# Downsampled attention values in 64x64 tiles of TensorE beside the local values in PSUM

## The chip, the cores and the metric

One core of one Trainium2 chip runs the whole program. The metric is device time in microseconds (us): the median of several executions of one kernel. The five engines that appear below are TensorE (PE; PEld is its loading of weights), VectorE (DVE), ScalarE (ACT), GpSimd (POOL) and SyncE (SP, which issues transfers).

## The reference

q, k and v have 8 batches, 8 heads, 576 positions and 64 columns. Two attentions are computed for each head and added: one over the means of 4 neighbouring positions (144 by 144), repeated 4 times, and one in which a position sees only positions at a distance below 4. A gated layer follows.

```
q_d, k_d, v_d = means of 4 rows            # 144 x 64 for each head
out_up    = repeat(softmax(q_d k_d' / 8) v_d, 4)
out_local = softmax(where(|i-j| < 4, q k' / 8, -1e9)) v
x = (out_up + out_local), heads side by side  # 8 x 576 x 512
h = relu(x @ w_in); u, v = halves of h     # w_in 512 x 1024
v_n = (v - mean) / sqrt(var + 1e-6)
v_s = w_spatial @ v_n + b_spatial          # over positions, 576 x 576
out = (u * v_s) @ w_out                    # w_out 512 x 512
```

## The kernel before

A step of attention, `attention(n)`, handles one pair of heads of one batch; there are 32 steps, n = 0 to 31, four for each batch. The two heads lie on partitions 0-63 and 64-127. After every four steps `gated(b)` lays out the gated layer of a batch, whose matmuls use all 128 rows and columns of the array in fp16 pairs of a high and a low part (batch 0 in fp32).

The pieces of one step on TensorE, with the names that the program gives them:

- S (line 875): 20 fp32 matmuls of 64 columns in the four 64x64 tiles of the array, the local scores. Where the mask is added on TensorE, four matmuls of line 868 precede them; otherwise VectorE adds it (line 888).
- Sd (line 922): 6 fp32 matmuls of 144 columns, the downsampled scores. A tile is diagonal where head h writes its own half of the partitions and off-diagonal where it writes the other half. Row block a = 0 and a = 1 use the two diagonal tiles, a = 2 the two off-diagonal ones; they are issued in the order 0, 2, 1.
- T (line 951) turns the local probabilities, Td (line 1013) the downsampled ones in fp16: nine matmuls with 112 moving columns.
- AV (line 1062): 20 fp32 matmuls of about 58 columns in 64x64 tiles, the local values, into the PSUM tile `pv`. Blocks 0, 2 and 4 use diagonal tiles, blocks 1 and 3 off-diagonal ones.
- AVd (line 1051): the downsampled values of batches 1 to 7, 10 fp16 matmuls with 96 rows and 64 columns of weights and 144 moving columns, five for each half of the output partitions, into the PSUM tile `pw`, a bank from the pool `pm` that the gated layer uses too.

ScalarE copies `pw` with a scale to `dn` (line 1084), VectorE adds it to `pv` (`both`, lines 1072 and 1074).

The order of all instructions is worked out before anything is emitted: class `Plan` keeps a list of pieces with a cost, a list `ORDER` of numbers that rank them, and a string per kind of choice in `ON` that says which engine takes it. `run` places the pieces by these, and each engine then runs its list in that order. From step 8 on, S, Sd of one step and AV, AVd of the step before are forced to follow each other without a gap (`first.next`, `second.next`, `av.next`); there are 24 such units. Below, such four pieces are called a unit, and Q, H and F are the ways in which the array is divided: 64x64 tiles, column halves, and whole. `TURN` holds the planner's cost of passing from one to another.

Of the kernel before, what the change touches and what calls it, by code (L numbers as in the profile page):

```python
# [76 lines left out]
class Plan:  # L77
# [64 lines left out]
    def run(self, near=150.0, stay=0.0, dma=(1500.0, 4.2, 500.0), emit=True):  # L142

        free = {}
        todo = {}
# [9 lines left out]
        for o in self.ops:  # L155
            free.setdefault(o.eng, 0.0)
            todo.setdefault(o.eng, [])
            if not o.wait:
                todo[o.eng].append(o)
# [264 lines left out]
MB = 8  # L424


ON = {"shrink": "AAAAAAADA",
      "sum": "PPDPDPDDPDDDPDPDDPPDDPPDPPDPPPDP",
      "mask": "TTTTTTDTDDTDDTDDDDTTD",
      "norm": "DPPPDPPDDPDPDDDDDPPDDDDPDDDPPPD",  # L430
# [923 lines left out]
```

## Time and profile before

| what | value |
|---|---|
| median of 3 runs | 568.89 us (568.71 to 569.19) |
| span of the profiled execution | 568.2 us |
| PE busy | 547.3 us, 96% of the span |
| DVE, ACT, POOL busy | 445.1, 362.8, 138.6 us |
| granted PE clock, mean | 0.979 of 2.4 GHz |

The page gives the profiled execution by its span alone, from the first to the last instruction; no other time of that execution is recorded, so its own time is taken as the span and stands 0.7 us below the median of the three runs. The span has three parts: up to about 68 us the inputs and weights come in and the first four steps run, to about 500 us attention and the gated layer are interleaved, and the rest is the gated layer of the last batch alone. A busy engine is not one at its peak; for TensorE the distance from the start of one piece to the start of the next is read, since records of consecutive matmuls overlap.

### The profile page before, as it was taken

The numbers are of one execution on the slowest core, as the hardware profiler recorded it, in microseconds if no ns is written. First come the engines' busy times: TensorE is split into PE (matmuls) and PEld (weight loads), VectorE is DVE, ScalarE is ACT, GpSimd is POOL, SyncE is SP. The second block draws the span as 40 slices with busy tenths as digits, with TensorE's granted clock in tenths as the row PEclk, the third lists the DMA queues.
The fourth block names the chain that finished last, engine by engine and source line by source line (L and its number), as shares of the span: only waits on it lengthen the run. The fifth ranks groups of instructions, "written<-read, shape, count | busy, mean of one in ns | idle before, by whom it ended". The sixth has DMA issues, their size and how long they took to land.

```text
span 568.2 us, 15639 instructions
## 1 busy us (share of the span) xinstructions
PE 547.3 (96%) x6312; PEld 368.1 (65%) x6312; DVE 445.1 (78%) x1222; ACT 362.8 (64%) x925; POOL 138.6 (24%) x163
## 2 busy tenths in 40 slices
PE   5878799999999999999999999999999999999997
PEld 2556367766777576766678566766767666865573
DVE  5789998996999888795799699899968878833350
ACT  4768787776775687555767678557755776544422
POOL 6314332201621123201521135203502132001300
PEclk9669899999999999999999999999999999999999
DMA  9999844215460445315342345332550410100102
GB/s 237 259 251 287 197 86 136 76 45 152 98 149 9 150 108 107 104 50 174 60 110 67 122 108 127 103 114 87 109 136 7 126 44 2 39 20 0 49 9 92
DMA packets 40467, 59.76 MB, mean 105 GB/s; under 512 B 4042, under 2 KB 27210, under 8 KB 40396
## 3 DMA queue, kind: packets, MB, share of 16 engines
q1 hardware_dynamic: 38092, 51.69, 31.5%
q0 software_dynamic: 2304, 7.08, 7.9%
q8 instruction: 49, 0.80, 0.7%
q14 instruction: 22, 0.18, 0.1%
HBM read 46.57 MB, written 9.44 MB: 99 GB/s over the span
## 4 chain that ended last, share of the span: by engine, by line
PE 81%; DVE 7%; DMA 7%; ACT 2%; POOL 1%; issue 1%; SPq 0%; ACTq 0%; DVEq 0%; POOLq 0%
PE pma L1257 5%; PE pmb L1220 5%; PE pmd L1220 5%; PE pmc L1257 5%; PE pmd L1257 4%; PE pma L1131 4%; PE pmb L1131 4%; PE pmd L1198 4%; PE pmb L1198 4%; PE pmc L1220 4%; PE pma L1220 3%; PE pmd L1131 3%; PE pma L1198 3%; PE pmc L1198 3%; PE pmb L1257 2%; PE pab L1062 2%
## 5 line engine op out<-in xcount | busy, mean ns | idle before, releaser
L1220 PEld LDWEIGHTS <-vha 128*128 128x128 f16 x768 | 73.7, 98 | 19.4
L1198 PEld LDWEIGHTS <-win 128*128 128x128 f16 x672 | 64.7, 98 | 18.8
L1257 PEld LDWEIGHTS <-more 128*128 128x128 f16 x192 | 18.6, 98 | 20.8
L1257 PEld LDWEIGHTS <-g 128*128 128x128 f16 x192 | 18.3, 98 | 20.4
L1220 PE MATMUL pmb<-wsp,vha 128*128 128x256 f16 (+1 forms) x228 | 30.9, 285 | 0.0
L1220 PE MATMUL pmd<-wsp,vha 128*128 128x256 f16 (+1 forms) x216 | 29.5, 286 | 0.0
L846 POOL TENSOR_TENSOR suma<-qkb 128x576 f32<-128x576 f32 x9 | 11.6, 1286 | 52.2 <-DMA qkb<-qk_dram 52.2
L1220 PE MATMUL pmc<-wsp,vha 128*128 128x320 f16 (+1 forms) x168 | 23.6, 290 | 0.0
L1162 POOL TENSOR_TENSOR stc<-stc,mhalf 128x1 f32<-128x1 f32 (+1 forms) x13 | 9.8, 753 | 54.6 <-DVE stc L1143 54.4
L846 POOL TENSOR_TENSOR suma<-qka 128x576 f32<-128x576 f32 x8 | 9.8, 1225 | 54.3 <-DMA qka<-qk_dram 50.3
L1162 POOL TENSOR_TENSOR stb<-stb,mhalf 128x1 f32<-128x1 f32 (+1 forms) x13 | 12.1, 934 | 44.5 <-DVE stb L1143 44.5
L1220 PE MATMUL pma<-wsp,vha 128*128 128x256 f16 (+1 forms) x156 | 20.8, 283 | 0.0
L943 POOL TENSOR_TENSOR sb<-sb,smb 128x640 f32<-128x640 f32 x9 | 12.3, 1364 | 28.0 <-DVE smb L910 17.2
L1162 POOL TENSOR_TENSOR sta<-sta,mhalf 128x1 f32<-128x1 f32 (+1 forms) x14 | 9.9, 705 | 28.8 <-DVE sta L1143 28.7
L1257 PE MATMUL pmd<-wo,g 128*128 128x512 f16 x72 | 16.5, 380 | 0.0
L1257 PE MATMUL pma<-wo,more 128*128 128x512 f16 x72 | 16.5, 379 | 0.0
L980 DVE SCALAR_TENSOR_TENSOR eh<-eda,smda,eh 128x144 f16<-128x144 f32 x42 | 15.9, 443 | 0.1
L980 DVE SCALAR_TENSOR_TENSOR wst<-edb,smdb,wst 128x144 f16<-128x144 f32 x42 | 15.0, 419 | 1.1 <-ACT wst L974 1.1
L765 POOL DMA_DIRECT2D tv<-v_dram x12 | 11.6, 970 | 14.1 <-DMA tv<-v_dram 13.9
L1131 PEld LDWEIGHTS <-xa 128*128 128x128 f16 x84 | 8.2, 98 | 9.9
L939 ACT ACTIVATE sa<-sa 128x640 f32<-128x640 f32 x16 | 11.8, 734 | 4.2 <-DVE sa L903 3.2
L939 ACT ACTIVATE sb<-sb 128x640 f32<-128x640 f32 x16 | 11.8, 738 | 3.4 <-DVE sb L894 1.8
(1051 smaller groups left out, 1713.1 us busy)
## 6 DMA issues: line engine op xcount, KB each, us to landing
qka<-qk_dram SPq DMA_DIRECT2D x16, 576.0 KB, 3.9
qkb<-qk_dram SPq DMA_DIRECT2D x16, 576.0 KB
tv<-v_dram POOLq DMA_DIRECT2D x12, 288.0 KB, 5.6
wst<-v_dram POOLq DMA_DIRECT2D x12, 288.0 KB, 5.0
stg<-w_in_dram SPq DMA_DIRECT2D x6, 512.0 KB, 6.2
out_dram<-rowa SPq DMA_DIRECT2D x8, 256.0 KB, 2.0
out_dram<-rowd SPq DMA_DIRECT2D x8, 256.0 KB, 4.9
out_dram<-rowc SPq DMA_DIRECT2D x7, 256.0 KB, 2.0
```

What stands on the lines that cost most here:

```text
L765: plan.op("POOL", 850, lambda r=r: nc.gpsimd.dma_start(t.ap, v4[b, r], accum_op=ALU.add), w=[t], rank=rank + 2.0 + 0.3 * r, kb=288, name="tv")
L846: side(s1).tensor_tensor(sb.ap.rearrange("p x (g r) -> p x g r", r=2), x[:, :, :, :2], x[:, :, :, 2:], op=ALU.add)
L939: exp_of.append(plan.op("ACT", 643, lambda: nc.scalar.activation(s.ap, s.ap, AF.Exp, scale=1.0 / 8.0), w=[s], rank=R["E"], name="exp"))
L943: plan.op(nm, 0, lambda: side(nm).tensor_tensor(s.ap, s.ap, sm.ap[:, :, None].broadcast_to([P, NW, 64]), op=ALU.mult), r=[sm], w=[s], rank ...
L980: nc.vector.scalar_tensor_tensor(eh.ap[:, a, :, 1], ed.ap[:, a, :], smd.ap[:, a:a + 1], eh.ap[:, a, :, 0], op0=ALU.mult, op1=ALU.subtract)
L1062: nc.tensor.matmul(pv.ap[h * 64:h * 64 + 64, c:c + QB[w + 1] - QB[w]], vb.ap[k, w], pT.ap[k, blk, q0:q0 + QB[w + 1] - QB[w]], start=True, ...
L1131: nc.tensor.matmul(ps.ap, xs[c].ap[:, i, t * P:(t + 1) * P], win[:, c, j, FF:], start=(c == 0 and (i, j) == (0, 0)), stop=(c == NC - 1 and ...
L1162: plan.op("POOL", 830, lambda: nc.gpsimd.tensor_tensor(st.ap[:r, 8:9], st.ap[:r, 8:9], mhalf[:r], op=ALU.pow), w=[st], rank=rank - EVICT, ...
L1198: nc.tensor.matmul(ps.ap[:, :n], win[:, c, i, ft * P:(ft + 1) * P], xs[c].ap[:, j, HA[h]:HA[h + 1]], start=(c == 0 and (i, j) == (0, 0)), ...
L1220: nc.tensor.matmul(ps.ap[:, :n], vh.ap[:, c, i, fs], wsp[:, c, j, hs], start=(c == 0 and (i, j) == (0, 0)), stop=False)
L1257: nc.tensor.matmul(ps.ap, g.ap[:, c, i, k:k + P] if t < NT else gt.ap[:, c, i], wo[:, c, j, :], start=(c == 0 and (i, j) == (0, 0)), stop= ...
```

## The change

The downsampled values are computed in 64x64 tiles, in four partial products: rows 0-63 and rows 64 up of the transposed probabilities meet their own half of `th` (now on 128 partitions, with another layout of rows), so that 16 matmuls take the place of 10. They write into the PSUM tile `pv`, at columns that the local values leave free: diagonal products into its first bank, off-diagonal ones into its second. A new VectorE instruction adds the second half to `dn`. In Sd, a = 1 and a = 2 are both off-diagonal and the order is 0, 1, 2. In a unit, AV has another order of blocks. Td transposes pieces with 128 instead of 96 weight columns. All numbers of `ORDER` and most choices in `ON` are new: 6 instead of 11 steps add the mask on TensorE (none of them in a unit; before, 4 were), 12 instead of 19 local normalisations and 11 instead of 19 low parts of v (line 1168) run on VectorE, the rest on POOL.

```diff
-            for a in (0, 2, 1):
+            for a in range(3):
...
-                    c = h ^ (a == 2)
+                    c = h ^ (a > 0)
...
-                    x = eh.ap[:112, a, 96:].rearrange("p k x -> p (k x)") if c == 1 else eh.ap[:112, a, :96, c // 2]
+                    x = eh.ap[:112, a, :P, c] if c < 2 else eh.ap[:112, a, 80:].rearrange("p k x -> p (k x)")
...
-        pw, dn = plan.buf("pm"), plan.buf("dn")
+        dn = plan.buf("dn")
+        def part_d(bank):
+            at = 512 * bank + (3 - bank) * BLK - 4 * (1 - bank)
+            return pv.ap[:, at:at + G]
...
-            passes = ((0, 0), (2, 0), (0, 2), (1, 1), (1, 3))
-            for i, (c, k) in enumerate(passes):
-                for h in range(2):
-                    nc.tensor.matmul(pw.ap[h * 64:h * 64 + 64, :G], w[:, k, p, h * D:h * D + D], t[:, c, :, h, :],
-                                     start=i == 0, stop=i == len(passes) - 1)
+            for i, (c, k) in enumerate(((0, 0), (0, 1), (1, 0), (2, 2), (2, 3))):
+                for cross_tile in range(2):
+                    for h in range(2):
+                        r = h ^ cross_tile
+                        if c == 2 and not r:
+                            continue
+                        rows = slice(64, P if c == 2 else 112) if r else slice(64)
+                        nc.tensor.matmul(part_d(cross_tile)[h * 64:h * 64 + 64], w[rows, k, p, h * D:h * D + D], t[rows, c, :, h, :],
+                                         start=i == 0, stop=i == (4 if r else 2))
...
+            if chained:
+                order = [(0, 0), (0, 1), (2, 0), (1, 0), (2, 1), (1, 1), (4, 0), (3, 0), (4, 1), (3, 1)]
...
+            if not whole:
+                plan.op("DVE", 220, lambda: nc.vector.scalar_tensor_tensor(dn.ap, part_d(1), sx_of[b][0].ap[:, 11:12], dn.ap, op0=ALU.mult, op1=ALU.add),
...
-      "mask": "TTTTTTDTDDTDDTDDDDTTD",
-      "norm": "DPPPDPPDDPDPDDDDDPPDDDDPDDDPPPD",
+      "mask": "DDTTTTTTDDDDDDDDDDDDDDDDDDDDDDDD",
+      "norm": "PPDPDPPPDDPPDPPPPPDPPDPPDDDPPDDP",
```

What the change does to the order is shown at two places. The first is TensorE's list at a unit in the middle of the program, before; L875 is S, L922 Sd, L1062 AV and L1051 AVd, whose pairs repeat to ten:

```order
L875 MATMUL paa<-qka 64x64 x20
L922 MATMUL pmc<-kda 64x144 x2
L922 MATMUL pmd<-kda 64x144 x2
L922 MATMUL pmc<-kda 64x144 x2
L1062 MATMUL pab<-probTb,vd 64x60 x2
L1062 MATMUL pab<-probTb,vd 64x58 x2
L1062 MATMUL pab<-probTb,vd 64x56 x2
L1062 MATMUL pab<-probTb,vd 64x58 x10
L1062 MATMUL pab<-probTb,vd 64x54 x2
L1062 MATMUL pab<-probTb,vd 64x58 x2
L1051 LDWEIGHTS wst
L1051 MATMUL pma<-pdTa,wst 64x144
```

The same unit in the changed kernel, where L900 is S, L947 Sd, L1101 AV and L1085 AVd, whose pairs repeat to sixteen:

```order
L900 MATMUL paa<-qka 64x64 x20
L947 MATMUL pma<-kda 64x144 x2
L947 MATMUL pmb<-kda 64x144 x4
L1101 MATMUL pab<-probTb,vd 64x60 x2
L1101 MATMUL pab<-probTb,vd 64x56 x2
L1101 MATMUL pab<-probTb,vd 64x58 x8
L1101 MATMUL pab<-probTb,vd 64x54 x2
L1101 MATMUL pab<-probTb,vd 64x58 x6
L1085 LDWEIGHTS wst
L1085 MATMUL pab<-pdTa,wst 64x144
L1085 LDWEIGHTS wst
L1085 MATMUL pab<-pdTa,wst 64x144
```

Sd now ends with two pairs into one bank, the off-diagonal ones, AV begins with three blocks of diagonal tiles (columns 60, 56 and 58), and AVd stays with the tile `pab` that AV writes.

The second place is VectorE's list behind a unit, before; L888 adds the mask of the new step, L925 to L927 and L891 take maxima, L1072 and L1074 add `dn` to the local values of the older step:

```order
L888 TENSOR_TENSOR sa<-paa,mask 128x2x3x64
L888 TENSOR_TENSOR sa<-paa,mask 128x2x2x64
L925 TENSOR_REDUCE mxda<-pmb 128x2
L926 TENSOR_REDUCE mxda<-pma 128x1
L927 TENSOR_SCALAR mxda<-mxda 128x3
L891 TENSOR_REDUCE mxa<-sa 128x10
L1072 TENSOR_TENSOR xfa<-pab,dnb 128x2x116 x2
L1074 TENSOR_TENSOR xfa<-pab,dnb 128x112
L894 TENSOR_TENSOR sa<-sa,mxa 128x640
```

A like place in the changed kernel, where L913 adds the mask, L950 to L952 and L916 take maxima, L1127 is the new instruction and L1111 and L1113 add `dn`:

```order
L913 TENSOR_TENSOR sb<-pab,mask 128x2x3x64
L913 TENSOR_TENSOR sb<-pab,mask 128x2x2x64
L950 TENSOR_REDUCE mxdb<-pmc 128x1
L951 TENSOR_REDUCE mxdb<-pma 128x2
L952 TENSOR_SCALAR mxdb<-mxdb 128x3
L916 TENSOR_REDUCE mxb<-sb 128x10
L1127 SCALAR_TENSOR_TENSOR dna<-paa,sxb,dna 128x144
L919 TENSOR_TENSOR sb<-sb,mxb 128x640
L1111 TENSOR_TENSOR xfb<-paa,dna 128x2x116 x2
L1113 TENSOR_TENSOR xfb<-paa,dna 128x112
```

The new instruction stands between a maximum and the subtraction (L919) that needs that maximum; what follows it in the list waits until it has run.

## Rows read from the trace of the kernel before

**Rows 1.** The page, part 1: busy time of each engine.
```profile
PE 547.3 (96%) x6312; PEld 368.1 (65%) x6312; DVE 445.1 (78%) x1222; ACT 362.8 (64%) x925; POOL 138.6 (24%) x163
```

**Rows 2.** The page, part 4: the chain that ended last, by engine.
```profile
PE 81%; DVE 7%; DMA 7%; ACT 2%; POOL 1%; issue 1%; SPq 0%; ACTq 0%; DVEq 0%; POOLq 0%
```

**Rows 3.** Busy time by stretch: length, PE, PEld, DVE, ACT, POOL, PEclk, DMA share, GB/s.
```profile
40.00:68.00 28.00, 23.32 (x273) 14.80 (x274) 27.23 (x75) 21.33 (x61) 8.62 (x10) 0.93 0.96 263
...
250.00:350.00 100.00, 99.60 (x1259) 68.17 (x1252) 82.41 (x225) 68.33 (x180) 28.42 (x30) 1.00 0.44 113
...
78.00:568.20 490.20, 485.02 (x5620) 330.48 (x5618) 381.18 (x1056) 309.41 (x782) 109.38 (x112) 1.00 0.32 85
```

**Rows 4.** PE's waits from 78 us on, the two longest of four: total, times, longest.
```profile
PE pmb L571 <- ACT junk L730: 0.4, 1, 0.4
PE pmb L1013 <- DVE eh L980: 0.4, 1, 0.4
```

**Rows 5.** Timeline of PE, the first unit: start, length, what, records; then the last unit's ends.
```profile
123.64 0.81 PE L875 MATMUL paa<-qka 64*64 64x64 f32 x40
124.28 0.29 PE L922 MATMUL pmb<-kda 64*64 64x144 f32 x2
...
124.52 0.29 PE L922 MATMUL pmb<-kda 64*64 64x144 f32 x2
124.54 0.33 PE L1062 MATMUL pab<-probTb,va 64*64 64x58 f32 x4
...
124.77 0.86 PE L1062 MATMUL pab<-probTb,va 64*64 64x60 f32 x36
125.56 0.50 PE L1051 MATMUL pma<-pdTa,th 96*64 96x144 f16 x10
125.99 0.82 PE L1257 MATMUL pmc<-wo,more 128*128 128x512 f16 x3
...
484.56 0.81 PE L875 MATMUL paa<-qkb 64*64 64x64 f32 x40
...
486.91 0.83 PE L1220 MATMUL pmc<-wsp,vha 128*128 128x256 f16 x6
```

**Rows 6.** Timeline of PE, a unit with the mask: its first piece and what follows it.
```profile
153.05 0.33 PE L868 MATMUL pab<-mask_b,mask_a 64*64 64x320 bf16 x4
...
155.51 0.58 PE L1198 MATMUL pmd<-xe,win 128*128 128x320 f16 x3
```

**Rows 7.** Timeline of PE, AV and AVd of the last step, outside a unit.
```profile
497.95 0.91 PE L1062 MATMUL paa<-probTb,vd 64*64 64x60 f32 x40
498.79 0.50 PE L1051 MATMUL pmd<-pdTa,th 96*64 96x144 f16 x10
499.22 0.99 PE L1220 MATMUL pma<-wsp,vha 128*128 128x320 f16 x6
```

**Rows 8.** Timeline of PE, the first of a Td's nine matmuls and what follows them.
```profile
320.02 0.26 PE L1013 MATMUL pmc<-ident,eh 112*96 112x112 f16 x2
...
320.46 0.39 PE L1198 MATMUL pmd<-xb,win 128*128 128x256 f16 x2
```

**Rows 9.** Groups by line and form, DVE and POOL: count, busy us, mean ns, idle before.
```profile
L980 DVE SCALAR_TENSOR_TENSOR eh<-eda,smda,eh 128x144 f16<-128x144 f32 x42 | 15.9, 443 | 0.1
L943 DVE TENSOR_TENSOR sa<-sa,sma 128x640 f32<-128x640 f32 x12 | 10.1, 844 | 0.2
...
L888 DVE TENSOR_TENSOR sa<-paa,mask 128x384 f32<-128x384 f32 x8 | 4.4, 548 | 0.6 <-PE paa L875 0.4
...
L926 DVE TENSOR_REDUCE mxdb<-pmc 128x1 f32<-128x144 f32 x6 | 1.8, 298 | 0.0
...
L943 POOL TENSOR_TENSOR sb<-sb,smb 128x640 f32<-128x640 f32 x9 | 12.3, 1364 | 28.0 <-DVE smb L910 17.2 <-PE paa L875 6.0 <-DVE kda L849 4.7
```

**Rows 10.** PE's waits over the whole span, the longest.
```profile
PE pab L951 <- POOL sb L943: 3.1, 1, 3.1
```

**Rows 11.** ScalarE's copy to `dn` (line 1084): idle before it, until when, and how often.
```profile
  PE pma L1051: 12.9, 10
```

More of the change, by code (lines that the diff above doesn't have):

```diff
@@ L142, in run @@
     def run(self, near=150.0, stay=0.0, dma=(1500.0, 4.2, 500.0), emit=True):
-        free = {}
-        todo = {}
+        free = dict.fromkeys(("SP", "DVE", "ACT", "PE", "POOL"), 0.0)
+        todo = {e: [] for e in free}
         port = 0.0
@@ L155, in run @@
         for o in self.ops:
-            free.setdefault(o.eng, 0.0)
-            todo.setdefault(o.eng, [])
             if not o.wait:
@@ L424 @@
 MB = 8
-ON = {"shrink": "AAAAAAADA",
-      "sum": "PPDPDPDDPDDDPDPDDPPDDPPDPPDPPPDP",
-      "mask": "TTTTTTDTDDTDDTDDDDTTD",
-      "norm": "DPPPDPPDDPDPDDDDDPPDDDDPDDDPPPD",
-      "normd": "PDAAPAAAPPAPAAAPAADAAADDDAAAAAAD",
-      "vlo": "DPDDDDPDDDDPDPDDPDPDDPPDDDPDDDDPPDDDPDP"}
+ON = {"shrink": "ADAAAADDAADA",
+      "sum": "PDDPPPPDPPDDPPPPDDPDDPDPPPDDDDDP",
+      "mask": "DDTTTTTTDDDDDDDDDDDDDDDDDDDDDDDD",
+      "norm": "PPDPDPPPDDPPDPPPPPDPPDPPDDDPPDDP",
+      "normd": "PAAAAAAAPPAPAADPAADAADAPAPAADAAP",
+      "vlo": "PPDPDPPDPDDPPDDDPDDDPPDDDPPDPDPPPPDPPPD"}
 @with_exitstack
@@ L518, in tile_kernel @@
     plan.tag("tv", [old[:72, :2 * FF].rearrange("p (j d) -> p j d", j=NP), tv1])
-    th1 = const.tile([96, 4, NP, 2 * D], F16, name="th1")
-    plan.tag("th", [old[:96, 2 * FF:4 * FF].bitcast(F16).rearrange("p (c j d) -> p c j d", c=4, j=NP), th1])
+    th1 = const.tile([P, 4, NP, 2 * D], F16, name="th1")
+    plan.tag("th", [old[:, 2 * FF:4 * FF].bitcast(F16).rearrange("p (c j d) -> p c j d", c=4, j=NP), th1])
     places("tx", 1, [72, 4, NP, 2 * D], F16)
@@ L534, in tile_kernel @@
     places("smd", 2, [P, 3], F32)
-    places("pdT", 1, [96, 2, 3, 96], F32)
+    places("pdT", 1, [P, 2, 3, 96], F32)
     places("dn", 2, [P, G], F32)
@@ L812, in spread_rows @@
         def spread_rows():
-            a, z = th.ap[:, ::2], tx.ap
-            for dst, src in ((a[:72], z[:, ::2]), (a[72:], z[:24, 1::2]), (th.ap[0:96:2, 1::2], z[24:, 1::2]), (th.ap[1:96:2, 1::2], z[24:, 1::2])):
+            a, z = th.ap, tx.ap
+            for dst, src in ((a[:72, :2], z[:, ::2]), (a[72:112, :2], z[:40, 1::2]), (a[64::2, 2:], z[40:, 1::2]), (a[65::2, 2:], z[40:, 1::2])):
                 nc.sync.dma_start(dst, src)
@@ L913, in down @@
         def down(a):
-            return pd[a // 2].ap[:, (a % 2) * G:(a % 2) * G + G]
+            return pd[min(a, 1)].ap[:, a // 2 * G:a // 2 * G + G]
         def scores_d():
             q = kb.ap.rearrange("p x g -> p (x g)")
-            for a in (0, 2, 1):
+            for a in range(3):
                 for h in range(2):
                     r = slice(h * 64, h * 64 + 64)
-                    c = h ^ (a == 2)
+                    c = h ^ (a > 0)
                     nc.tensor.matmul(down(a)[c * 64:c * 64 + 64], q[r, 48 * a:48 * a + 64], kb.ap[r, 1], start=True, stop=True)
         def maximum_d():
-            nc.vector.tensor_reduce(mxd.ap[:, :2], pd[0].ap[:, :2 * G].rearrange("p (a k) -> p a k", a=2), axis=AX.X, op=ALU.max)
-            nc.vector.tensor_reduce(mxd.ap[:, 2:], down(2), axis=AX.X, op=ALU.max)
+            nc.vector.tensor_reduce(mxd.ap[:, :1], down(0), axis=AX.X, op=ALU.max)
+            nc.vector.tensor_reduce(mxd.ap[:, 1:], pd[1].ap[:, :2 * G].rearrange("p (a k) -> p a k", a=2), axis=AX.X, op=ALU.max)
             nc.vector.tensor_scalar(mxd.ap, mxd.ap, -1.0 / 128.0, None, op0=ALU.mult)
@@ L930, in attention @@
         first = plan.op(sc, 0, scores, r=[qkb], w=[ps], hold=[s, *([*pd, ed, *prev[1]] if prev else ())], after=prev[2] if prev else (), rank=R["S"], mode="Q", name="S")
-        second = plan.op("PE", 510, scores_d, r=[kb], w=list(pd), hold=[ed], after=[first] if prev else (), rank=R["Sd"], lag=PEL, mode="Q", name="Sd")
+        second = plan.op("PE", 330 if prev else 510, scores_d, r=[kb], w=list(pd), hold=[ed], after=[first] if prev else (), rank=R["Sd"], lag=PEL, mode="Q", name="Sd")
         if prev:
@@ L996, in turn_d @@
                 for a in range(3):
-                    nc.tensor.matmul(v[:, a, :112], ed.ap[:112, a, kc * 72:kc * 72 + n], cross if a == 2 else ident[:112, :112],
+                    nc.tensor.matmul(v[:, a, :112], ed.ap[:112, a, kc * 72:kc * 72 + n], cross if a else ident[:112, :112],
                                      start=True, stop=True, is_transpose=True)
@@ L1008, in turn_h @@
         def turn_h():
-            v = turned(ptd[0])[:96, :9 * 112].rearrange("p (c a q) -> p c a q", c=3, a=3)
+            v = turned(ptd[0])[:, :9 * 112].rearrange("p (c a q) -> p c a q", c=3, a=3)
             for c in range(3):
                 for a in range(3):
-                    x = eh.ap[:112, a, 96:].rearrange("p k x -> p (k x)") if c == 1 else eh.ap[:112, a, :96, c // 2]
-                    nc.tensor.matmul(v[:, c, a], x, cross16 if a == 2 else ident16, start=True, stop=True, is_transpose=True)
+                    x = eh.ap[:112, a, :P, c] if c < 2 else eh.ap[:112, a, 80:].rearrange("p k x -> p (k x)")
+                    nc.tensor.matmul(v[:, c, a], x, cross16 if a else ident16, start=True, stop=True, is_transpose=True)
         def half_t():
@@ L1019, in copy_h @@
             nc.scalar.copy(half_t().rearrange("p (c q) -> p c q", q=96),
-                           turned(ptd[0])[:96, :9 * 112].rearrange("p (c q) -> p c q", q=112)[:, :, :96])
+                           turned(ptd[0])[:, :9 * 112].rearrange("p (c q) -> p c q", q=112)[:, :, :96])
         copies = [copied]
@@ L1041, in values_d @@
                 for kc, n in enumerate(KEYS):
-                    nc.tensor.matmul(pw.ap[h * 64:h * 64 + 64, :G], tv.ap[:, p, (2 * kc + h) * D:(2 * kc + h + 1) * D], t[:n, kc, :, h, :],
+                    nc.tensor.matmul(part_d(0)[h * 64:h * 64 + 64], tv.ap[:, p, (2 * kc + h) * D:(2 * kc + h + 1) * D], t[:n, kc, :, h, :],
                                      start=(kc == 0), stop=(kc == 1))
@@ L1047, in values_h, with values @@
             w = th_of[b].ap
-            passes = ((0, 0), (2, 0), (0, 2), (1, 1), (1, 3))
-            for i, (c, k) in enumerate(passes):
-                for h in range(2):
-                    nc.tensor.matmul(pw.ap[h * 64:h * 64 + 64, :G], w[:, k, p, h * D:h * D + D], t[:, c, :, h, :],
-                                     start=i == 0, stop=i == len(passes) - 1)
-        def values():
-            order = [(blk, i, h) for j in range(0, NBLK, 2) for i in range(2) for blk in (j, j + 1) for h in range(2) if blk < NBLK]
-            for blk, i, h in order:
+            for i, (c, k) in enumerate(((0, 0), (0, 1), (1, 0), (2, 2), (2, 3))):
[7 more added lines that the diff above has]
+                                         start=i == 0, stop=i == (4 if r else 2))
+        def values(chained):
+            if chained:
+                order = [(0, 0), (0, 1), (2, 0), (1, 0), (2, 1), (1, 1), (4, 0), (3, 0), (4, 1), (3, 1)]
+            else:
+                order = [(blk, i) for j in range(0, NBLK, 2) for i in range(2) for blk in (j, j + 1) if blk < NBLK]
+            for blk, i, h in [(*o, h) for o in order for h in range(2)]:
                 w = 2 * blk + i
@@ L1077, in finish @@
         def finish(*after):
-            av = plan.op("PE", 675, values, r=[vb, pT], w=[pv], hold=[xf, x], after=after, rank=R["AV"], lag=PEL, mode="Q", name="AV")
-            avd = plan.op("PE", 450 if whole else 240, values_d if whole else values_h,
-                          r=[*((tv,) if whole else (th_of[b].sub(0),)), pdT.sub(0), pdT.sub(1)], w=[pw], hold=[dn], after=[av] if after else (), rank=R["AVd"], lag=PEL, mode="H", name="AVd")
+            av = plan.op("PE", 560 if after else 675, lambda: values(bool(after)), r=[vb, pT], w=[pv], hold=[xf, x], after=after, rank=R["AV"], lag=PEL, mode="Q", name="AV")
+            avd = plan.op("PE", 450 if whole else 190 if after else 260, values_d if whole else values_h,
+                          r=[*((tv,) if whole else (th_of[b].sub(0),)), pdT.sub(0), pdT.sub(1)], w=[pv.sub("d")], hold=[dn], after=[av] if after else (), rank=R["AVd"], lag=PEL,
+                          mode="H" if whole else "Q", name="AVd")
             if after:
                 av.next = avd
-            plan.op("ACT", 176, lambda: nc.scalar.copy(dn.ap, pw.ap[:, :G]) if whole else
-                    nc.scalar.activation(dn.ap, pw.ap[:, :G], AF.Copy, scale=sx_of[b][0].ap[:, 11:12]),
-                    r=[pw, *(() if whole else (sx_of[b][0].sub(10),))], w=[dn], rank=R["AVd"] - EVICT, name="dn")
-            plan.op("DVE", 795, both, r=[pv, dn], w=[x.sub(0) if whole else xf], rank=R["AV"] - EVICT, name="xf")
+            plan.op("ACT", 176, lambda: nc.scalar.copy(dn.ap, part_d(0)) if whole else
+                    nc.scalar.activation(dn.ap, part_d(0), AF.Copy, scale=sx_of[b][0].ap[:, 11:12]),
+                    r=[pv.sub("d"), *(() if whole else (sx_of[b][0].sub(10),))], w=[dn], rank=R["AVd"] - EVICT, name="dn")
+            if not whole:
+                plan.op("DVE", 220, lambda: nc.vector.scalar_tensor_tensor(dn.ap, part_d(1), sx_of[b][0].ap[:, 11:12], dn.ap, op0=ALU.mult, op1=ALU.add),
+                        r=[pv.sub("d"), sx_of[b][0].sub(10)], w=[dn], rank=R["AVd"] - EVICT, name="dn2")
+            plan.op("DVE", 795, both, r=[pv, pv.sub("d"), dn], w=[x.sub(0) if whole else xf], rank=R["AV"] - EVICT, name="xf")
             if whole:
```

273 rows, old and new, of the table ORDER are left out of this document.

## The prediction

> **What bounds the kernel now.** I read the busy times first: PE is busy for 96% of the span and the next engine, DVE, for 78% [rows 1]. A busy share alone proves nothing, so the chain that ended last comes second: 81% of it is PE's own work, 7% DVE and 7% transfers [rows 2]. Third, the stretches: from 78 us to the end PE is busy in 485.0 of 490.2 us, at a granted clock of 1.00 (the 2.4 GHz level) [rows 3], and its waits in all that time are four, the two longest 0.4 us each [rows 4]. The reader should see a queue that is never empty: there, a microsecond of work taken from PE is a microsecond of the span, until another engine falls behind. DVE, with 82.4 us in a steady 100 [rows 3], is the nearest. The stretch before differs: from 40 to 68 us DVE has 27.2 of 28 us and the transfers 0.96, and PE idles [rows 3].
>
> Last, PE's timeline gives the price of a unit [rows 5]. In the first one S starts at 123.64, Sd at 124.28, AV's main part at 124.77, AVd at 125.56 and the next piece at 125.99: 2.35 us. All 24 units cost the same (2.34 or 2.35 without mask, the last 484.56 to 486.91), and four of them add a mask, 153.05 to 155.51, 2.46 us [rows 6]. So one number times 24 carries the sum.
>
> **The change part by part.** *Sd, AV and AVd in a unit.* From Sd's start to the next piece is 1.71 us now [rows 5]. Two of Sd's three pairs share the diagonal tiles, 0.24 us each (124.28 to 124.52). AV's main part then takes 0.79 us, of which its first four records ran early, at 124.54, in the other tiles. AVd costs 0.43. A Td gives the price of one fp16 pass: nine with 112 columns in 0.44 us [rows 8], 0.049 each, hence 0.063 for 144 columns and 0.31 for five; what is left of AVd's 0.43, 0.12 us, I take as the emptying of the array before another division. The new unit is bounded from three rows.
>
> - A, tile by tile. S puts five blocks of 64 columns through each tile in 0.64 us, 0.128 each, so 0.116 for 58 columns. The diagonal tiles do one pair of Sd and six blocks, 0.24 + 6 x 0.116 = 0.94; the others two pairs and four blocks, 0.48 + 0.46 = 0.94. The changed list lets these run side by side. The tiles with rows from 64 up then do five passes, 0.31, and the array empties, 0.12: 1.37 us, 0.34 less than now.
> - B, issue alone. S has 40 records in 0.64 us, 0.016 each. Sd, AV and AVd will have 12 + 40 + 16 = 68 records: 1.09 + 0.12 = 1.21 us, 0.50 less.
> - C, every matmul of the program at S's 0.032 (20 in 0.64). AVd's sixteen then need 0.51 instead of 0.31: 1.57 us, 0.14 less.
>
> I take 1.29, the middle of A and B, 0.42 less: A charges each block the pace of four busy tiles, which part of the new unit doesn't have, and B is below what the tiles' own work allows. C counts a pace that S shows only with two records for a matmul. So 24 x 0.42 = 10.1 us less, with ends of 12.0 and 3.4.
>
> *The mask.* Four units lose it, 4 x 0.11 = 0.4 us less. The other move is among the first eight steps.
>
> *Lone AVd.* Four steps have theirs outside a unit, 0.43 us after an AV of 0.84 [rows 7]. Five passes and one emptying come out the same; the emptying between AV and AVd goes, at most 4 x 0.12. I take 0.
>
> *Td.* It loads 128 weight columns instead of 96, in 28 steps x 9. If its pace is that of the 112 moving columns, this is free; if it goes with the weights, each costs a third of 0.049 more, 252 x 0.016 = 4.0 us. The pace is just that of the columns, so I take 0.5. The Trainium skill ("TensorE: Matmul & The Clock Gate", section "LDWEIGHTS (loading the stationary operand)") speaks against the change here: loading time goes with the number of weight columns, 1.2 columns a nanosecond, so 96 would need 80 ns. The trace has 49 ns for load and pass together and disagrees with the figure; by the rule's direction alone the sum would be 3.5 us worse.
>
> *VectorE.* The new instruction runs 28 times. The nearest rows are a reduction of 144 columns from PSUM, 0.30 us, and the three-operand form on 144 columns, 0.44 [rows 9]: 8 to 12 us. Five more masks cost 0.55 and, for the smaller part, by columns 0.37: 4.6. Seven normalisations go, 7 x 0.84 = 5.9, and eight subtractions of 512 columns, at that pace 0.68: 5.4. Net 2 to 6 us on an engine with 109 us free after 78 us [rows 3]. I cost it at nothing; the cover is that free time, some 2.5 us in each of the 15 us from unit to unit.
>
> *The wait that is added.* The instruction needs ScalarE's copy, which needs AVd, and ScalarE already stands idle for PE there, 12.9 us in 10 cases in one tile's group [rows 11], 1.3 us each. What queues behind it on VectorE is the subtraction and, through exp, sum and normalisation, the next T. Even if it stalls that long each time, 1.3 + 0.4 is under the 2.5 us of free time.
>
> *POOL.* It takes the seven normalisations, 1.36 us there against 0.84, and the eight subtractions, about 18 us more on 109 in 490 [rows 3, 9]. PE's longest wait of all is for such a normalisation, 3.1 us before 68 us [rows 10]. I allow 0.5 us for new waits.
>
> *The rest.* The bank of `pw` comes free, but PE waits for no bank now. The four transfers that spread `th` stay four, on SP's queue, of other row counts. Copies of 128 instead of 96 partitions have the same columns. The first 68 us keep the order of the weight transfers, but DVE has more masks at once: 0, with 2 us either way.
>
> *Sum.* 568.2 - 10.1 - 0.4 + 0.5 + 0.5 = 558.7 us of span. The median stands 0.7 us above the profiled span, so 559.4 us, **9.5 us less** than 568.9.
>
> **The rivals.** *C, issue of matmuls.* For it: S's 0.032 for a matmul and AVd's own 0.031 (ten in 0.31) are close, as if no matmul came faster. Against: S's records come at 0.016, and AVd's 0.031 is also what two column halves give. Then 568.9 - 3.4 - 0.4 + 1 = 566 us; halfway 563. The Trainium skill has a rule of this kind ("TensorE: Matmul & The Clock Gate", section "Wait — 56ns, not 53.3ns?"): matmuls never start closer than about 25 ns. The trace agrees if a matmul of two records counts as one and disagrees if each record does; by the rule AVd takes 0.40 us and the time is some 2 us above my forecast.
>
> *POOL late, the side on which it gets slower.* More of the normalisations that T needs lie on POOL, 20 instead of 13, each 0.5 us longer, and PE takes its list in order. For it: the one wait of 3.1 us [rows 10]. Against: none after 78 us [rows 4], and POOL is idle for 72% of the steady stretch [rows 3]. It decides from the point where the new waits of PE exceed 9.5 us, four like that one; with five, 15.5 us, the time is 568.9 - 10 + 15.5 = 574 us.
>
> *The tiles don't overlap.* If off-diagonal Sd, AV and AVd run after one another as before, only the emptying between AV and AVd goes, 24 x 0.12 = 2.9 us, and a start that is 2 us longer leaves 568 us, no change. Against: four records of AV did start while Sd's third pair ran [rows 5].
>
> **How the numbers follow.** The forecast, from A to B, has a chance of 0.70; C and what lies halfway to it 0.16; POOL late 0.09; no overlap 0.03; better than B 0.02. The time is that of the likeliest, 559.4. B with a start 2 us shorter gives 568.9 - 12.0 - 0.4 - 2 = 554.5; C is 566. The range 555 to 566 leaves out the two last rivals and little else. About 0.2% or 1.1 us is what a measurement of this kernel can tell from no change. Faster has 0.70 + 0.16 + 0.02 = 0.88; no change 0.03; slower 0.09.
>
> **What would show it.** In the changed profile S to the next piece should be 1.93 us (A 2.01, B 1.85, C 2.21) in all 24 units and no mask among them; PE should have fewer busy microseconds by about 10 and no wait above 1 us after 78 us; a Td should stay at 0.44 to 0.48; DVE should be near 447 to 451 us busy, POOL near 157. The prediction is wrong if a unit costs over 2.2 us, if PE's waits after 78 us exceed 3 us, or if PE is continuously busy from a point over 3 us later than now.

## The result and the profile after

The changed kernel takes 574.07 us (median of 4 runs, 573.46 to 574.93) beside 569.04 us of the kernel before on the same chip: a ratio of 1.0085, with a 95% interval of 1.0068 to 1.0102. It is **slower by 5 us** where 9.5 us less were forecast. Its profiled execution has a span of 572.0 us, 3.8 us more than that of before, while the medians lie 5.0 us apart. The two profiles don't stand alike to their medians. The changed kernel's execution took 573.9 us, 1.9 us more than its span. In the runs further below, executions of the kernel before took 2.1 us more than their spans (568.97 us with a span of 566.9, for one). By that its profiled execution, with a span of 568.2 us, took about 570.3 us, an estimate: above the median and not, as taken ahead of the prediction, 0.7 us below it. So about 1.2 of the 5.0 us are not in these two profiles.

Busy time and the chain that ended last, of the changed kernel (parts 1 and 4 of the page), beside [rows 1, 2]:

```profile
PE 538.6 (94%) x6459; PEld 359.2 (63%) x6459; DVE 451.4 (79%) x1241; ACT 361.6 (63%) x922; POOL 156.1 (27%) x180
PE 79%; DVE 11%; ACT 3%; DMA 3%; POOL 1%; issue 1%; SPq 0%; POOLq 0%; DVEq 0%; ACTq 0%
```

TensorE has 8.7 us less to do, and yet the span is longer. So its idle time must have grown by 12.5 us, and the first question is where. Two stretches of each kernel answer it (columns as in [rows 3]); first of the kernel before, then of the changed one:

```profile
0.00:80.00 80.00, 64.26 (x698) 38.21 (x699) 65.74 (x178) 54.67 (x147) 29.62 (x52) 0.85 0.92 230
80.00:568.20 488.20, 483.02 (x5616) 329.92 (x5614) 379.38 (x1045) 308.14 (x779) 109.00 (x111) 1.00 0.32 85
```
```profile
0.00:80.00 80.00, 60.82 (x719) 35.72 (x720) 66.69 (x177) 53.30 (x146) 29.12 (x50) 0.85 0.92 241
80.00:572.00 492.00, 477.79 (x5741) 323.51 (x5739) 384.73 (x1066) 308.32 (x776) 127.01 (x131) 0.99 0.31 82
```

Idle is the length less PE's busy time: in the first 80 us 15.7 before and 19.2 now, after that 5.2 before and 14.2 now. The larger part, 9.0 us, comes in the stretch that [rows 4] showed to be almost without waits (1.4 us in all). TensorE's waits from 78 us on, in the changed kernel (total, times, longest):

```profile
PE pmd L1038 <- DMA wst<-txa: 3.3, 1, 3.3
PE pab L976 <- POOL sa L968: 2.1, 2, 1.3
PE paa L1085 <- DMA th<-txa: 1.8, 1, 1.8
PE pmd L1241 <- ACT ua L1247: 1.6, 1, 1.6
PE pmb L602 <- DVE sxb L599: 0.4, 1, 0.4
```

They sum to 9.2 us. A single one, the Td at line 1038 behind the transfers that spread `th`, is longer than all four waits of before together. The unit itself did what it should. TensorE's timeline at the first unit, and at a Td (the rows that answer to [rows 5, 8]):

```profile
127.47 0.81 PE L900 MATMUL pab<-qka 64*64 64x64 f32 x40
128.10 0.29 PE L947 MATMUL pmc<-kda 64*64 64x144 f32 x2
...
128.34 0.22 PE L1101 MATMUL paa<-probTb,va 64*64 64x60 f32 x2
...
129.04 0.50 PE L1085 MATMUL paa<-pdTa,th 64*64 64x144 f16 x16
129.47 1.90 PE L1300 MATMUL pmb<-wo,more 128*128 128x512 f16 x8
...
326.27 0.21 PE L1038 MATMUL pmb<-ident,eh 112*128 112x112 f16 x1
...
326.72 0.81 PE L1174 MATMUL pmc<-win,xb 128*128 128x512 f16 x3
```

From S to the next piece are 2.00 us, in 23 of the 24 units 2.00 or 2.01. The one that differs, at 459.21, has the wait of 1.8 us inside it, in the middle of its AVd: twelve of the records run, the last four wait for the transfer of `th` that was issued at 457.08. The row of SyncE's queue, then those of TensorE:

```profile
457.08 3.26 SPq L840 DMA_DIRECT2D th<-txa  x4
```
```profile
460.78 0.39 PE L1085 MATMUL paa<-pdTa,th 64*64 64x144 f16 x12
462.93 0.31 PE L1085 MATMUL paa<-pdTa,th 64*64 64x144 f16 x4 [1.76 <-DMA th<-txa]
```

The longest wait is stranger. SyncE issues four transfers into a `th` buffer at 116.96; VectorE, at line 1005, writes the remainder of the downsampled probabilities (what is left of them after the high part) into `eh` and is held until the transfers land; Td, which reads this `eh`, is released by the same landing, and all behind it in TensorE's list waits with it. Timeline of SyncE's queue, VectorE and TensorE, in this order (the bracket gives the idle time ahead and what ended it):

```profile
116.96 3.31 SPq L840 DMA_DIRECT2D wst<-txa  x4
...
118.62 0.20 DVE L844 TENSOR_SCALAR sx2a<-sw,sxa 128x1 f32<-128x1 f32 x1
121.89 0.94 DVE L1005 SCALAR_TENSOR_TENSOR wst<-eda,smda,wst 128x144 f16<-128x144 f32 x3 [3.07 <-DMA wst<-txa]
...
121.93 0.21 PE L1038 MATMUL pmd<-ident,wst 112*128 112x112 f16 x1 [3.29 <-DMA wst<-txa]
...
123.09 4.44 PE L1300 MATMUL pma<-wo,g 128*128 128x512 f16 x12
...
129.47 2.76 PE L1300 MATMUL pmb<-wo,more 128*128 128x512 f16 x12
```

The remainder step doesn't read what the transfers bring. But the first of the two `eh` buffers and the first of the two `th` buffers are parts of one tile, `wst`, the old place of the spatial weights, and both rows carry its name. The last two rows show a second price: one piece O (line 1300, the product with `w_out` at the end of the gated layer) took 4.44 us right after the wait, and its like 2.76 us a little later. The stretches around it give the reason in their granted clock (the first of the last three figures):

```profile
120.00:122.00 2.00, 0.07 (x2) 0.10 (x3) 0.11 (x1) 0.00 (x0) 0.00 (x0) 1.00 0.28 66
122.00:124.00 2.00, 1.80 (x12) 0.87 (x12) 2.00 (x6) 0.65 (x1) 0.00 (x0) 0.83 0.00 0
124.00:126.00 2.00, 2.00 (x6) 0.75 (x5) 2.00 (x7) 1.21 (x3) 0.00 (x0) 0.50 0.00 0
126.00:128.00 2.00, 2.00 (x41) 0.91 (x43) 1.41 (x4) 1.07 (x4) 0.00 (x0) 0.82 0.02 4
128.00:130.00 2.00, 2.00 (x91) 1.66 (x84) 1.55 (x6) 0.82 (x3) 0.00 (x0) 1.00 0.36 50
```

It was still 1.00 (the 2.4 GHz level) while TensorE stood idle for 3.3 us, and then fell to 0.50 (the 1.2 GHz level) for a while. So this one dependency costs 3.3 + 1.7 = 5.0 us in this profile.

### The profile page after: what moved, and what is told of

The parts are those of the page before. It is cut to its first block, busy times and chain, and to the rows that moved or that the text cites. A ratio compares the mean times of both kernels' runs of the same rounds, so it can differ in the third digit from the quotient of the medians.

```text
span 572.0 us, 15981 instructions
## 1 busy us (share of the span) xinstructions
PE 538.6 (94%) x6459; PEld 359.2 (63%) x6459; DVE 451.4 (79%) x1241; ACT 361.6 (63%) x922; POOL 156.1 (27%) x180
## 4 chain that ended last, share of the span: by engine, by line
PE 79%; DVE 11%; ACT 3%; DMA 3%; POOL 1%; issue 1%; SPq 0%; POOLq 0%; DVEq 0%; ACTq 0%
PE pma L1300 5%; PE pmd L1300 5%; PE pmb L1263 4%; PE pma L1263 4%; PE pmb L1300 4%; PE pmc L1263 4%; PE pmd L1174 4%; PE pmd L1241 4%; PE pmd L1263 3%; PE pmc L1241 3%; PE pma L1241 3%; PE pma L1174 3%; PE pmc L1174 3%; PE pmb L1241 2%; PE paa L1101 2%; PE pab L900 2%
## 5 line engine op out<-in xcount | busy, mean ns | idle before, releaser
L968 POOL TENSOR_TENSOR sb<-sb,smb 128x640 f32<-128x640 f32 x12 | 15.6, 1297 | 54.6 <-DVE smb L935 45.0
L1263 PE MATMUL pmb<-wsp,vha 128*128 128x256 f16 (+1 forms) x216 | 28.2, 280 | 0.0
L1263 PE MATMUL pma<-wsp,vha 128*128 128x256 f16 (+1 forms) x204 | 27.6, 285 | 0.0
L1263 PE MATMUL pmd<-wsp,vha 128*128 128x320 f16 (+1 forms) x168 | 23.5, 289 | 0.0
L968 POOL TENSOR_TENSOR sa<-sa,sma 128x640 f32<-128x640 f32 x8 | 10.7, 1337 | 39.9 <-ACT rowb L1195 15.2
L1300 PE MATMUL pma<-wo,g 128*128 128x512 f16 x72 | 18.2, 408 | 0.0
L1005 DVE SCALAR_TENSOR_TENSOR wst<-eda,smda,wst 128x144 f16<-128x144 f32 x39 | 13.7, 415 | 3.1 <-DMA wst<-txa 3.1
L1001 POOL TENSOR_TENSOR wst<-eda,smda 128x432 f16<-128x432 f32 x6 | 6.2, 1040 | 31.2 <-ACT sb L964 14.8
L1351 PE MATMUL pma<-mask_b,mask_a 128*128 128x512 bf16 x29 | 11.4, 547 | 3.0 <-DVE sw L693 3.0
L1300 PE MATMUL pmd<-wo,g 128*128 128x512 f16 x60 | 13.8, 379 | 0.0
```

The lines of the kernel that those rows point to most:

```text
L968: plan.op(nm, 0, lambda: side(nm).tensor_tensor(s.ap, s.ap, sm.ap[:, :, None].broadcast_to([P, NW, 64]), op=ALU.mult), r=[sm], w=[s], rank ...
L1005: nc.vector.scalar_tensor_tensor(eh.ap[:, a, :, 1], ed.ap[:, a, :], smd.ap[:, a:a + 1], eh.ap[:, a, :, 0], op0=ALU.mult, op1=ALU.subtract)
L1263: nc.tensor.matmul(ps.ap[:, :n], vh.ap[:, c, i, fs], wsp[:, c, j, hs], start=(c == 0 and (i, j) == (0, 0)), stop=False)
L1300: nc.tensor.matmul(ps.ap, g.ap[:, c, i, k:k + P] if t < NT else gt.ap[:, c, i], wo[:, c, j, :], start=(c == 0 and (i, j) == (0, 0)), stop= ...
L1351: nc.tensor.matmul(ap.rearrange("p (j k) -> p j k", k=64), mask_a, mask_b[:, None, :].broadcast_to([P, 8, 64]), start=True, stop=True)
```

## The experiments

The first theory, **order**: the tiles give their 8 us, and what took them back is the new order, which puts some steps too close behind what they need. Its rival, **tiles**: the new code brings its waits along wherever it stands. In all runs the planner is replaced by a list, so that an order can be kept or altered step by step (`SEQ` is the list of steps, `SLOT` the buffers that they get, `ON` the engines). With the changed kernel's own list, as in run 2, each engine has as many instructions as in the changed kernel (6459, 1241, 922 and 180 on PE, DVE, ACT and POOL). The lines then stand some 120 lines further up: 1005 becomes 882 to 884. Each ratio below is to the kernel before, run beside it on the same chip (568.97 us for runs 1 to 4, 569.0 for run 5, 569.41 for runs 6 to 8).

```diff
     def run(self, near=150.0, stay=0.0, dma=(1500.0, 4.2, 500.0), emit=True):
-        while left:
...
+        for step, i in enumerate(SEQ):
+            o = self.ops[i]
...
+                    b.slot = int(SLOT[b.tag][b.number])
...
+            o.fn()
```

**1. New tiles in the old sequence.** `SEQ`, `SLOT` and `ON` are those of the kernel before.

> The code of the change (64x64 tiles, halves added on VectorE, scores mostly on off-diagonal tiles) with every instruction at the place that it has in the kernel before: the planner is replaced by the list of steps and buffers that the kernel before got, and the added VectorE step stands right ahead of the xf step that reads it (five steps near 95 us stand a little differently, since one bank is used otherwise). Theory 'order': the tiles gain what the changed kernel's units show, 24 x 0.34 = 8.2 us, and 0.4 us of masks may or may not come with it, so 569.0 - 8.2 = 561 us (559 to 563), and what lost the time is the new order. Rival 'tiles': the tiles bring their waits along wherever they stand (a transfer of 128 rows that lands late, the extra VectorE step, VectorE work bunched by shorter units): 569 us or more.

Measured: 567.25 us, ratio 0.9972 (0.9950 to 0.9994). Neither theory is met: 1.7 us less, not 8, and not none. The trace, of an execution of 570.16 us, shows where the gain goes. Its first unit starts at 126.68 and its last at 485.15, where before had 123.64 and 484.56 [rows 5]: 360.9 us before, 358.5 now, so of the 7.8 us that the 23 units in between save (0.34 each) only 2.4 are left. TensorE's five longest of thirteen kinds of waits from 78 us on, 7.2 us together where before had 1.4:

```profile
PE pmb L915 <- DVE eh L882: 1.1, 1, 1.1
PE pmd L1118 <- ACT ug L1124: 0.9, 1, 0.9
PE paa L853 <- DVE sa L845: 0.8, 2, 0.5
PE pma L473 <- ACT uc L1124: 0.8, 1, 0.8
PE pab L962 <- DVE sb L805: 0.7, 1, 0.7
```

All are short, and all but 0.2 us for VectorE and ScalarE. I read this as TensorE coming too early for a list in which the other engines' steps stood just in time for the slower units; no run tests this reading by itself. The old order doesn't suit the new tiles, so the comparison can't hold the order fixed; each needs one made for it.

**2. `eh` in a tile of its own**, the changed kernel's order kept.

```diff
-    plan.tag("eh", [old[:, 4 * FF:4 * FF + 3 * G].bitcast(F16).rearrange("p (a k x) -> p a k x", a=3, x=2), eh1])
+    eh0 = const.tile([P, 3, G, 2], F16, name="eh0")
+    plan.tag("eh", [eh0, eh1])
...
```

> The changed kernel with its own order, but the first of the two buffers for the normalized downsampled probabilities (eh) is a tile of its own and no longer lies in the tile of the spatial weights, where the first th buffer lies too. Theory 'shared tile': VectorE's 3.1 us of waiting at 118.6 us for the th transfer, TensorE's 3.3 us behind it and the clock that falls to 0.67 after it come only from the two buffers sharing one tile, since the transfer and the remainder step touch different bytes: the wait goes, and with it 3.3 us and about 1.7 us of slower clock, 574.1 - 5 = 569 us (568 to 571). Rival 'needed': the step behind it needs the transfer or something as late: 573.5 to 574.5 us.

Measured: 568.26 us, ratio 0.9990 (0.9970 to 1.0011), against 1.0085 of the changed kernel: by the ratios 5.4 us less, as expected. The same place, VectorE and then TensorE:

```profile
118.36 0.20 DVE L722 TENSOR_SCALAR sx2a<-sw,sxa 128x1 f32<-128x1 f32 x1
118.48 0.92 DVE L883 SCALAR_TENSOR_TENSOR eh<-eda,smda,eh 128x144 f16<-128x144 f32 x3
...
119.67 2.75 PE L1178 MATMUL pma<-wo,g 128*128 128x512 f16 x12
122.36 0.81 PE L778 MATMUL pab<-qka 64*64 64x64 f32 x40
```

VectorE goes on without a wait, O takes 2.75 us, and the first unit starts at 122.36 instead of 127.47. The shared tile is shown to be the cause of the longest wait. Other waits, of 6.8 us together, stay in this order.

**3. The late transfer sent earlier**, on top of run 2. The numbers are places in the program: 1726 is the scale, 1727 to 1730 half, thi, tlo and move.

```diff
-SEQ = [..., 1726, ..., 1727, ..., 1728, ..., 1729, ..., 1730, ...]
+SEQ = [..., 1726, 1727, ..., 1728, ..., 1729, ..., 1730, ..., ...]
```

> As the run with eh in a tile of its own, and for batch 7 the four steps that make and send the downsampled values (half, thi, tlo, move) stand right behind the scale that they read, some 35 steps of the list earlier, so that the transfer issued at 457.1 us goes some 9 us sooner. Theory 'late transfer': the 1.8 us that the AVd inside unit 22 waits for it goes: 1.8 us less than the run without the early move (567 if that is 569). Rival: the earlier VectorE and ScalarE work (1.4 and 1.1 us) delays something else that TensorE waits for, or the time comes back later as the end is set by the last rows: no change against that run.

Measured: 568.11 us, ratio 0.9985 (0.9963 to 1.0006): no change that the medians can tell from run 2, as the rival had it. The wait for `th` is gone from the trace, as TensorE's longest waits from 78 us on show, first of run 2 and then of run 3:

```profile
PE paa L963 <- DMA th<-txa: 2.0, 1, 2.0
```
```profile
PE pmd L1119 <- ACT ua L1125: 1.6, 1, 1.6
```

From 80 us to the end TensorE is idle for 7.9 us instead of 11.6, but waits that the edit doesn't touch went too: 1.5 us for a normalisation on POOL and 0.7 for ScalarE. And the first 80 us, in which the two runs have the same steps in the same order, differ the other way (PE idle for 20.6 us instead of 18.2). The start varies from execution to execution by more than this effect, so it is seen in the trace, and its worth in time isn't shown.

**4. Without the added halves.**

```diff
-                plan.op("DVE", 220, lambda: nc.vector.scalar_tensor_tensor(dn.ap, part_d(1), sx_of[b][0].ap[:, 11:12], dn.ap, op0=ALU.mult, op1=ALU.add),
+                plan.op("DVE", 220, lambda: None,
```

> The changed kernel with its own order but without the 28 added VectorE steps (the values on the off-diagonal tiles are left out of the downsampled output). Theory 'order': VectorE has slack there, and the steps cost nothing: 573.5 to 574.5 us. Rival 'VectorE': 28 steps of 0.35 us are about 10 us of VectorE's time, and if they delay what TensorE waits for, up to 5 us or more comes back: 564 to 569 us.

This kernel leaves out the off-diagonal half of the downsampled values. Measured: 572.95 us, just below the 573.5 to 574.5 us of the theory, ratio 1.0074 (1.0050 to 1.0097), not to be told from 1.0085. In this order the added VectorE steps cost nothing that can be measured, although they are 28 x 0.36 us; the 5 us or more of the rival are ruled out.

**5. Another order.** The steps of the change, listed by the kernel's own planner after its durations had been put right by the traces and its numbers in `ORDER` and letters in `ON` had been varied for as long as the planned end fell. `eh` and `th` have tiles of their own.

```diff
+    th0 = const.tile([P, 4, NP, 2 * D], F16, name="th0")
-    plan.tag("th", [old[:, 2 * FF:4 * FF].bitcast(F16).rearrange("p (c j d) -> p c j d", c=4, j=NP), th1])
+    plan.tag("th", [th0, th1])
...
-      "norm": "PPDPDPPPDDPPDPPPPPDPPDPPDDDPPDDP",
+      "norm": "PDPPPPDPDPDPDDDPDPDPPPDDDDPDDPDP",
```

> The code of the change (same tiles, same steps) in another order and with other engines for the steps that may run on either: a list of steps found by the same kind of planning, but with the durations that the traces show (the AVd of a unit 0.1 us longer, 3.3 us for issuing the four th transfers and 5.8 us until they have landed, some 3 to 5% more for VectorE, more slack behind VectorE, ScalarE and GpSimd), with the start taken from the kernel before as a first guess, and with both eh buffers and both th buffers in tiles of their own. Theory 'order': the tiles' 8.2 us are there once no piece of TensorE waits, so TensorE waits for under 3 us in all after 80 us, idles no more than before in the start (16 to 18 us), and the time is 569.0 - 8 - 1 = 560 us (556 to 563). Rival 'VectorE is as near to full as TensorE': as in the run with the old sequence, the waits come back elsewhere whatever the order, since VectorE is busy 85 of 100 us: 565 to 570 us.

Measured: **561.52 us**, ratio 0.9868 (0.9844 to 0.9891). TensorE's waits from 78 us on, then its two stretches:

```profile
PE pmd L917 <- DVE eh L884: 1.1, 1, 1.1
PE pab L980 <- ACT dnb L1003: 0.3, 1, 0.3
PE pmd L475 <- DVE ue L1159: 0.2, 1, 0.2
```
```profile
0.00:80.00 80.00, 62.94 (x738) 37.75 (x739) 68.08 (x179) 58.16 (x155) 27.21 (x49) 0.87 0.91 241
80.00:559.80 479.80, 473.06 (x5731) 321.56 (x5729) 381.16 (x1068) 305.30 (x775) 113.52 (x119) 1.00 0.31 84
```

1.6 us of waits are left, and 17.1 us of idle time in the start. The rival on VectorE falls: VectorE is about as busy as in the changed kernel (449.2 and 451.4 us), and the waits didn't come back. But this run differs from run 2, with its 6.8 us of waits, in the order and in the engines at once (POOL is busy for 140.7 us here and for 156.7 there), so how much belongs to which isn't shown.

**6. The control: old tiles, an order looked for in the same way** (`SEQ`, `SLOT` and all of `ON` differ, one line of it here; tiles as in run 5).

```diff
-      "norm": "DPPPDPPDDPDPDDDDDPPDDDDPDDDPPPD",
+      "norm": "PDPPDPPPDPDDPDPPDDDPDDPDDPPPPDP",
```

> The code of the kernel before (AVd in column halves with its own bank, no added VectorE step) in an order that was looked for in just the way of the run with the other order: same durations, same slack, same time of looking, its own old sequence as the first guess, eh and th in tiles of their own. It tells how much of that run's gain belongs to the tiles and how much to a better order. Theory 'tiles': the order before was already without waits after 80 us (four, of 0.4 us at most), so nothing is left to win, and the tiles are worth what the units show: 568 us (566 to 570), 6 to 9 us above the run with the other order. Rival 'order': another order would have gained as much without the tiles: 560 to 564 us.

Measured: 568.74 us, ratio 0.9977 (0.9952 to 1.0001). Nothing is won. The two stretches:

```profile
0.00:80.00 80.00, 63.10 (x766) 38.23 (x767) 68.69 (x173) 54.50 (x147) 26.43 (x47) 0.83 0.89 241
80.00:567.70 487.70, 483.14 (x5530) 330.43 (x5528) 382.42 (x1061) 305.45 (x770) 108.05 (x113) 1.00 0.31 83
```

From 80 us on TensorE is busy for 483.1 us, as in the kernel before (483.0), and idle for 4.6. With the old tiles these 4.6 us are all that an order could still win in this stretch, and one search didn't win them; run 5 is 10.1 us of work below it in the same stretch.

**7. A second order with the new tiles**, found by going on from that of run 5 (again one line of what differs).

```diff
-      "norm": "PDPPPPDPDPDPDDDPDPDPPPDDDDPDDPDP",
+      "norm": "PDPPPPDPPPPPPPDPPPDDDDPPPPPDDPPD",
```

> The code of the change in a second order, found by going on from the first other order with the same durations and slack. Theory: an order that leaves TensorE without waits is not one lucky list; the time is within 2 us of the first (559.5 to 563.5 us). Rival 'luck': the first was a lucky one, and another with the same slack on paper lands at 565 us or more.

Measured: **557.6 us**, ratio 0.9802 (0.9776 to 0.9827), the best of all. The rival, luck, falls, but the time is 3.9 us from run 5 and not within 2. Its waits from 78 us on:

```profile
PE pab L855 <- DVE sb L847: 0.5, 1, 0.5
PE pab L855 <- POOL sb L847: 0.3, 1, 0.3
PE pmb L917 <- ACT edb L863: 0.2, 1, 0.2
```

They are 1.0 us together, 0.6 less than in run 5. More of the difference is in TensorE's busy time, 531.5 us against 536.0, and 2.6 us of that are matmuls of line 1230 that compute nothing, with which the program keeps TensorE busy during the start: 15 records, 5.6 us in all, in place of 25 with 8.2. So not all of this gain is the tiles', and there is no run with the old tiles and a search as long.

**8. The order of run 5 with the shared tile back** (the diff of run 2 and the lines on `th` of run 5 undone).

> The first other order with eh and th back in the tile of the spatial weights, as in the kernel before and the changed one. Theory 'place decides': the shared tile costs only where a remainder step happens to stand close behind a th transfer; in this order some of the 14 that use the shared buffer may, so 561.5 to 566 us. Rival 'the tile alone': the shared tile costs what it did in the changed kernel, 5 us or more, whatever the order: 566.5 us or more.

Measured: 561.33 us, ratio 0.9874 (0.9846 to 0.9903), as run 5 and just below the theory's 561.5 to 566 us. In its trace the first remainder step into the shared `eh` starts at least 14 us after the first transfer into the shared `th` (378.37 and 392.94 are the closest), and none waits for a transfer. The shared tile costs nothing where no remainder step stands close behind a transfer; it costs 5 us in the order of the changed kernel. So the tile alone is not the cause, but the tile together with the place that the order gives.

## Why the prediction was wrong

*What bounded the kernel* was read rightly. With TensorE's waits away, the time follows TensorE's work: before, run 6 and run 5 have 547.3, 546.2 and 536.0 us of it in spans of 568.2, 567.7 and 559.8. That runs 5 and 7, at 561.5 and 557.6 us, lie on either side of the 559.4 us forecast is no proof of the sum: they have other orders and engines than the kernel forecast, and the largest term was off.

*The unit.* 2.00 us: that is bound A (2.01), where 1.93 was taken. The gain is 24 x 0.34 = 8.2 us instead of 10.1, a term mis-sized by 1.9 us. A was left because part of the unit doesn't keep four tiles busy; but Sd and AV together take 0.94 us (128.10 to 129.04) and AVd 0.43, just A's figures. The tiles do work side by side, as the Trainium skill has it ("TensorEngine Tiling (Array Packing)", section "Key Properties": tiles operate independently), and by A's sum what fills the time is the tiles' own work and not the issue of matmuls. Rival C (2.21) is out.

*The mask* is gone from the units. *Td* stays at 0.45 us with 128 weight columns (0.44 before): the 0.5 us allowed were not needed. The Trainium skill's rule that loading goes with the columns ("TensorE: Matmul & The Clock Gate", section "LDWEIGHTS (loading the stationary operand)") doesn't show in these rows. The records of the loads alone go the other way: 124 ns for 96 columns at line 1013 of the kernel before, 98 for 128 at line 1038 (medians). *VectorE*, forecast 447 to 451 us, has 451.4, and run 4 shows no cost of the added steps that can be measured. *POOL*, forecast near 157 us, has 156.1.

*The step that failed* is the one called the rest: "The four transfers that spread `th` stay four, on SP's queue, of other row counts", costed at 0. It named neither who waits for them nor what hides them. Two wait: the AVd that reads `th`, and, through the shared tile, the remainder step on VectorE with the Td behind it. What hid them was the distance that the old order kept between a transfer and these steps. In the kernel before, no AVd starts less than 8 us after the first transfer of its `th` (318.78 and 326.92 are the closest), where the changed kernel has 3.7 at one place (457.08 and 460.78); and the shared `eh` is next written more than 20 us after a transfer into the shared `th`, here at the first of them (SyncE's queue, then VectorE):

```profile
122.75 4.22 SPq L815 DMA_DIRECT2D wst<-txa  x4
...
145.66 0.92 DVE L980 SCALAR_TENSOR_TENSOR wst<-edb,smdb,wst 128x144 f16<-128x144 f32 x3
```

The change replaces every number of that order. The price was 3.3 + 1.7 us at 121.9 us, shown by run 2, and a wait of 1.8 us at 462.9, which run 3 took away in the trace without a gain in the medians.

Behind it stands a reading that was too wide. That TensorE had hardly waited after 78 us [rows 4] was taken as a trait of the kernel; it was a trait of that order for those durations. Run 1 shows it from the other side: the same old order with shorter units waits in many small places. So "I allow 0.5 us for new waits" was too little even for what it covered: two waits for normalisations on POOL took 2.1 us, and one for ScalarE at a bank of U (line 1241, the product with `w_in`) 1.6 us, which no part of the prediction had. No run tests these waits by themselves.

*The start*, costed at 0 with 2 us either way, has 3.4 us more idle time in the profiles. How much of this is the new order is open: runs 2 and 3 have the same start and differ by 2.4 us, and the profiled execution of before was itself probably slower than its median. The last 1.1 us are at the end, as two rows show (before, with its end at 568.2, then changed, with its end at 572.0): TensorE is busy in all but 3.8 us of what is left from 540 us on before, in all but 4.8 us now.

```profile
540.00:575.00 35.00, 24.44 (x152) 14.55 (x149) 7.60 (x19) 7.13 (x17) 0.00 (x0) 0.98 0.12 39
```
```profile
540.00:575.00 35.00, 27.16 (x175) 16.82 (x172) 7.99 (x20) 7.94 (x18) 0.00 (x0) 0.95 0.14 46
```

*The rival that got slower*, POOL late, gave 574 us, and 574.07 was measured, but it isn't what happened: POOL has 2.1 of the 9.2 us. The number was met by another cause, which is luck. The prediction's own condition for being wrong, waits of over 3 us after 78 us, did name the sign to look for.

The sum, from the profiles: 8.7 us less work (in which 1.7 us of slow clock are lost), 7.9 us more waits between 80 and 540 us (9.0 less the 1.1 at the end), 3.4 us in the start and 1.1 at the end make 3.7 of the 3.8 us of longer span.

## What to carry to other kernels

When a change comes with a new order, the old trace can vouch for prices and not for waits: list each transfer and each step on another engine that TensorE's pieces need, and look in the new order at how far ahead of its reader it stands. Buffers of different use that lie in one tile can make steps wait for each other that share no data; where memory allows, give them tiles of their own. And judge a faster piece only in an order made for it, with an order made in the same way for the old piece as a control: here the tiles were worth 6 to 7 us (run 6 against runs 5 and 8; run 7 adds 4 us, but by a longer search, which the old tiles didn't have), and neither the old order nor the first new one showed it.

## What was not expected of the hardware

A wait can cost more than its length. In the changed kernel TensorE was idle for 3.3 us at 121.9, and O then took 4.44 instead of 2.76 us; after the waits of 1.8 us at 462.9 and 1.6 at 164.9 the granted clock stayed at 1.00. The Trainium skill ("TensorE: Matmul & The Clock Gate", section "Why this matters for your kernels") advises against long idle gaps between bursts of matmuls for this reason, and the trace agrees with its direction. The price isn't fixed: in the profile of run 4, which keeps the shared tile, the same wait is 2.9 us, the granted clock is 0.50 from 122 to 128 us, and O takes 5.22.

Four small transfers are slow to send: they occupy SyncE's queue for 3.3 us, and their last bytes could be used 4.9 to 5.8 us after the first was issued (116.96 to 121.89, 457.08 to 462.9), where the planner's table charges 1.8 us for the issue.

Sixteen fp16 matmuls in four tiles follow each other fast: the AVd of a unit, with the emptying of the array behind it, takes 0.43 us (129.04 to 129.47), as long as the ten in column halves did [rows 5].
